# Second block of chunk 1 as seven block products, with chunk 0's feature tiles run through and two weight conversions exchanged

## The chip, the cores and the metric

The kernel runs on one core of a Trainium2 chip. The metric is device time in microseconds (us), the median of several runs. A core has a matrix engine (PE), a vector engine (DVE), a scalar engine (ACT), a general engine (POOL) and a queue for transfers (SP). Each works through its own instructions in the order of the program and waits for the others by semaphores. PE writes to PSUM banks; everything else lies in SBUF.

## The reference

Attention with sketched features, followed by a two-layer network on its result. For each head, features of 64 numbers are made from q and k, and the output of attention is a ratio of two products with sums over the sequence:

```python
def phi(x):
    a = np.einsum('rd,bhsd->bhsr', S1, x)
    b = np.einsum('rd,bhsd->bhsr', S2, x)
    return np.einsum('bhsi,bhsj->bhsij', a, b).reshape(*x.shape[:-1], r * r)
kv = np.einsum('bhsf,bhsd->bhfd', k_p, v)
z = np.sum(k_p, axis=2)
num = np.einsum('bhsf,bhfd->bhsd', q_p, kv)
den = np.einsum('bhsf,bhf->bhs', q_p, z)[..., None] + 1e-06
# (num / den) becomes x: 4352 tokens of 128 channels
h = x @ w_in                                   # 128 x 2048
g = 0.5 * h * (1.0 + erf(h * inv_sqrt2))
return (g @ w_out).astype(np.float32)          # 2048 x 128
```

Batch 4, heads 4, sequence 1088, head size 32. The weights of S1, S2, w_in and w_out arrive as float64; everything is computed in float32.

## The kernel before

**Chunks and feature tiles.** The tokens are cut into eight chunks of 512 (n = 0 to 7, two for each batch entry) and a ninth of 256 with the rests. The hidden layer has 16 tiles of 128 features (fi = 0 to 15). For one pair (n, fi) the function `hidden` makes one product of w_in's tile with the chunk's x on PE (L683, into one of two PSUM banks `h_ps`), and ACT takes the bank through Gelu into SBUF (L690). A PSUM bank can be written again only when its Gelu has read it, so the hidden product of a step waits for the Gelu of two steps before.

**Two ways of the second product.** "Usual" tiles are multiplied with w_out's tile one by one (`project`, L818, a product of 128x128 by 128x512) and accumulate in a PSUM bank `o_ps`; ACT later copies that sum away (`take_usual`, L795). The other tiles are taken in blocks of four: `two_products` (L767) makes seven block products instead of eight, in a scheme of Winograd's kind. They are issued as seven pairs of 64x256 products for two tiles and two halves. The block products need two kinds of sums made on POOL beforehand: `token_sums` (L732 to L735, four instructions over the Gelu outputs of the block, into tiles `bits_low`, `bits_a`, `bits_e`, `bits_m`) and `channel_sums(i)` (L719 to L722, four instructions over piece i of w_out). In the order of the pairs, names 4 and 7 use `bits_low`, 1 and 5 `bits_a`, 6a and 6b `bits_e`, and 2 and 3 `bits_m`. When a chunk's last block is done, `drain` (L775 to L788) recombines the products on ACT and DVE, and `store` writes the chunk out.

**Conversion of the weights.** w_in and w_out come in five pieces each, of 2, 2, 4, 4 and 4 feature tiles (`w_in_sb[0]` to `[4]`). A piece is converted from float64 words by `Rounding`: ACT scales the low words (L260); DVE cuts out the exponent field (L268) and the mantissa field (L273); ACT makes the exponent (L279); DVE makes the mantissa (L287), sets the sign (L292), and DVE or, for some pieces, POOL multiplies (L297). `round_at(t, w)` puts the first half of this into step t and the second half into step t + 1.

**The order of the work.** It is written out by hand. A list `steps` gives the pairs (n, fi) in turn; for step t the loop at the end issues the hidden product and Gelu of its pair, then `token_sums` if a block is complete, then what `at(t, ...)` has put into the slot of t, then the second products due at t. An engine keeps exactly this order. Two lists matter here: the one of steps, and the one of slots (L988 to L1050), which holds the conversions, the channel sums and the attention of the next batch entry: turning keys (`key_turn_blocks`, L359), features (`features_of_all` L934, `outer_of_all` L942 to L949), their sums (`add_tokens`, L958 to L964), `finish_keys` (L428), `turn_kv` (L458), `z_sum`, `query_sketch` (L568), `query_outer` (L580 to L603), `attend` (L617).

Before the change the steps are: chunk 0 fi 0 to 3, chunk 1 fi 0 to 3, chunk 0 fi 4 to 7, chunk 1 fi 4 to 7 (all usual, steps 0 to 15), then chunk 0 fi 8 to 15 (steps 16 to 23), chunk 1 fi 8 to 15 (24 to 31), and from step 32 on the other chunks, with all their tiles in blocks. The conversions stand at steps 4 (w_in, piece 2), 6 (w_out, 2), 8 (w_in, 3), 10 (w_out, 3), 12 (w_in, 4) and 14 (w_out, 4).

Of the kernel before, what the change touches and what calls it, by code (L numbers as in the profile page):

```python
# [16 lines left out]
def kernel(  # L17
# [18 lines left out]
    pe, dve, act, pool, sp = nc.tensor, nc.vector, nc.scalar, nc.gpsimd, nc.sync  # L36
# [5 lines left out]
    NF = d_ff // 128  # L42
# [7 lines left out]
    NCH = J // JC  # L50
    C = D + 1
    LAG = 2
    NMAIN = B * NCH
    NB = 4

    USUAL = 8
    NCHUNK = NMAIN + 1
    assert B == 4 and d_model == 128 == H * D == JC * D == 2 * F and H == 4 and REM == 64 and NCH == 2

# [34 lines left out]
    w_in_sb = [big.tile([d_model, c1 - c0], FP, name=f"w_in{i}") for i, (c0, c1) in enumerate(pieces)]  # L94
# [92 lines left out]
    for i, s in enumerate((S1, S2)):  # L187
        s, e = words(s)
# [266 lines left out]
    def turn_kv(b, banks):  # L455

        for rows in (slice(0, 64), slice(64, 128)):
            pe.matmul(banks[rows, 1, :128], lhsT=kv_T[b], rhs=ident, start=True, stop=True)  # L458
        act.copy(out=kz[b], in_=banks[:, 1, :128])
# [217 lines left out]
    def hidden(n, fi, by_halves=False):  # L677
        W = width[n]
        ps = first_banks.pop((n, fi)) if (n, fi) in first_banks else hidden_bank()
        w = w_tile(w_in_sb, fi)  # L680
        for rows in (slice(0, 64), slice(64, 128)) if by_halves else (slice(0, 128),):
            if (n, fi) not in begun:
                pe.matmul(ps[rows, :W], lhsT=w[:, rows], rhs=xT[n][:, :W], start=True, stop=True)  # L683
        if n < NCH and fi < USUAL:
            g_of[n, fi] = mlp.tile([128, CW], FP, name="g", bufs=4)
        else:
            if fi % NB == 0:
                blocks[n, fi // NB] = block(FP)
            g_of[n, fi] = blocks[n, fi // NB][:, fi % NB]
        act.activation(out=g_of[n, fi][:, :W], in_=ps[:, :W], func=ACT.Gelu)  # L690
# [58 lines left out]
        return sums[n, b][j][:, e], T[j][:, k]  # L749

    def first_block(n):
        return USUAL // NB if n < NCH else 0

    def two_products(n, b, i):

        fours, ones_, sixes = [("4", "7", e, e) for e in range(2)], [("1", "5", e, e) for e in range(2)], ("6a", "6b", 0, 1)

        opens = b == first_block(n)
        order = fours + ([sixes] + ones_ if opens else ones_ + [sixes]) + [("2", "3", e, e) for e in range(2)]
        two = order[i]  # L760
        if opens and i == 0:
            acc[n] = [out_bank(), out_bank()]
        for name, e in zip(two[:2], two[2:]):
            half, bank, col = PLACE[name]
            moving, fixed = factor(n, b, name, e)

            pe.matmul(acc[n][bank][half * 64:(half + 1) * 64, col:col + HW], lhsT=fixed, rhs=moving,  # L767
                      start=opens and e == 0 and name in "4715", stop=b == NF // NB - 1, skip_group_check=True)
# [24 lines left out]
    def take_usual(n):  # L793
        usual[n] = mlp.tile([128, CW], FP, name="g", bufs=4)
        act.copy(out=usual[n], in_=o_of[n])  # L795
# [9 lines left out]
        return N[:, 1]  # L805

    def project(n, fi, parts=range(B // 2)):
        first, final = fi == 0, fi == (USUAL if n < NCH else NF) - 1
        if first:
            o_of[n] = out_bank() if n < NMAIN else [work_bank() for i in range(B // 2)]  # L810
        g = g_of[n, fi]
        if n == NMAIN:

            for i in parts:
                pe.matmul(o_of[n][i][:, :128], lhsT=g[:, i * 128:(i + 1) * 128], rhs=w_tile(w_out_sb, fi),  # L815
                          start=first, stop=final)
            return
        pe.matmul(o_of[n], lhsT=w_tile(w_out_sb, fi), rhs=g, start=first, stop=final)  # L818
# [65 lines left out]
    late = []  # L884
# [32 lines left out]
    w_out[0].fields()  # L917


    steps = [(n, fi) for f in range(0, USUAL, 4) for n in range(NCH) for fi in range(f, f + 4)]  # L920
    steps += [(n, fi) for n in range(NCHUNK) for fi in range(USUAL if n < NCH else 0, NF)]
    slots = {t: [] for t in range(len(steps) + LAG)}

    def at(t, f, *a):
        slots[t].append(lambda: f(*a))
# [40 lines left out]
    held = {}  # L966
# [21 lines left out]
    def round_at(t, w, product_by=dve):  # L988
        r = []
        at(t, lambda: (r.append(Rounding(w)), r[0].low_words(), r[0].fields()))  # L990
        at(t + 1, lambda: (r[0].exponents(), r[0].mantissas(), r[0].signs(), r[0].product(product_by)))

    for i, (t0, t1) in enumerate(((4, 6), (8, 10))):
        round_at(t0, w_in_sb[i + 2])
        round_at(t1, w_out_sb[i + 2])
    round_at(12, w_in_sb[4], pool)
    at(13, channel_sums, 3)

    at(12, widen_v_rem, 1)
    for r in range(2):  # L1000
        at(14, key_turn_blocks, 1, r)
    round_at(14, w_out_sb[4], pool)
    at(15, query_turn, 2)
    at(16, features_of_all, 1)
    at(16, outer_of_all, 1)
    at(16, turn_keys_rem, 1)
    at(17, features_rem, 1)
    at(17, add_tokens, 1)
    at(18, channel_sums, 4)

    at(21, finish_keys, 1, False)
    at(22, lambda: turn_kv(1, held["kv"]))
    at(23, z_sum, 1)
    at(23, fold_z, 1)
    at(23, query_turn, 3)
    at(24, query_sketch, 2)
    at(24, query_outer, 2)
    for i, t in enumerate((25, 26, 28)):
        at(t, channel_sums, i)
    at(11, spread_sketches)  # L1020
    at(40, repeat_first_z)
# [32 lines left out]
    done = {t: [] for t in range(len(steps) + LAG + 1)}  # L1054
    drains = {t: [] for t in range(len(steps) + LAG + 1)}
    for t, (n, fi) in enumerate(steps):
        if n < NCH and fi < USUAL:
            products[t + LAG].append((project, n, fi))
            if fi == USUAL - 1:
                slots[t + LAG + 1 + 2 * n].append(lambda n=n: take_usual(n))  # L1060
        elif n == NMAIN:
            at_ = max(t + LAG, (n * NF + 5) if fi < 3 else (n * NF + 6) if fi < 5 else 0)
            if fi < NF - 4:
                products[at_].append((project, n, fi))
            if fi == NF - 1:

                products[at_] += [(project, n, NF - f, (i,)) for f, i in ((4, 0), (3, 0), (2, 0), (4, 1), (1, 0), (3, 1),
                                                                          (2, 1), (1, 1))]
                done[at_ + 1].append(n)
        elif fi % NB == NB - 1:  # L1070
            b = fi // NB
            opens = b == first_block(n)
            late = int(n < NCH or n == NCH and opens)
            for later, pairs in ((3, 3), (4, 2), (5, 2)) if opens else ((2, 2), (3, 2), (4, 1), (5, 2)):
                later += late
                for i in range(pairs):
                    products[t + later].append((two_products, n, b, len([p for q in products.values() for p in q
                                                                        if p[:3] == (two_products, n, b)])))
            if b == NF // NB - 1:
                drains[t + 6 + late].append(n)  # L1080
                done[t + 12].append(n)

    for t in range(len(steps) + LAG):
        if t < 4:

            hidden(0, t)
            if t == 1:
                w_out[0].low_words()
                w_out[0].exponents()
                w_out[0].finish()  # L1090
                w_out[1].fields()
            if t == 2:
                w_out[1].low_words()
            if t == 3:
                banks = work_banks()
                numerators_by_token(1, halves(banks), range(JC))
                w_out[1].mantissas(by_pool=True)
                w_out[1].exponents()
                divide(1, banks, range(JC), by_head_pair=False)
                w_out[1].signs()  # L1100
                w_out[1].product()
                for u in range(4):
                    for f, *a in products[u]:
                        f(*a)
            continue
        if t == 4:
            for i, copy in enumerate((by_act, by_dve)):
                turn_half(1, i, work_bank(), copy)
            first_hidden(1, 0)
            for f, *a in products[t]:  # L1110
                f(*a)
            first_hidden(1, 1)
        for n in drains[t]:
            drain(n)
        if t < len(steps):
            n, fi = steps[t]
            hidden(n, fi, by_halves=t >= 18 and (n < NMAIN or fi < 5))
        if t < len(steps) and steps[t][0] < NMAIN and steps[t][1] % NB == NB - 1:
            n, b = steps[t][0], steps[t][1] // NB
            if b >= first_block(n):  # L1120
                token_sums(n, b)
        for f in slots[t]:
            f()
        for n in done[t]:
            store(n)
        if t != 4:
            for f, *a in products[t]:
                f(*a)
# [41 lines left out]
```

## Time and profile before

| what | value |
|---|---|
| device time, median of 3 runs | 262.52 us (262.11 to 262.53) |
| the profiled execution's own time | 261.87 us |
| its span, first to last instruction | 260.1 us |
| PE busy | 255.2 us, 98% of the span |
| POOL busy | 163.4 us, 63% |
| DVE busy | 152.2 us, 59% |
| ACT busy | 114.6 us, 44% |
| granted PE clock | full in all slices |

The profile is of one execution. Its page gives the busy time of each engine, the span in 40 slices with a digit of tenths, the chain of work that ended last, and the costliest groups of instructions. A row of the timeline gives start, duration, engine, line of the kernel, operation, output and inputs, shape and count, and in brackets the idle time of the engine just before with what ended it. The rows' durations overlap a little on one engine, so the time from one start to the next is the better price of an instruction. All times are us from the start of the span. A matmul on float32 shows as two records; two products on the two halves of PE's columns run side by side.

The steps that the change touches lie between 29 and 75 us. Step t = 8 (chunk 0, fi 4) begins on PE at 29.20, step 16 at 42.94 and step 20 at about 49.4.

### The profile page before, as it was taken

Reading aid. Unit: us, or ns where it says so; the run is one execution under the profiler, and the core shown is the slowest. Engines: PE = TensorE matmul, PEld = TensorE weight load, DVE = VectorE, ACT = ScalarE, POOL = GpSimd, SP = SyncE. Lnnn points to the kernel's source line nnn. Section 1 sums busy time; section 2 is a strip of 40 time slices with the busy share of each in tenths; the row PEclk is TensorE's granted clock in tenths of the full one; section 3 lists DMA queues with packets and bytes.
Section 4 is the critical chain, followed back from the end, with each engine's and each line's share of the span. In section 5 each row is a group of like instructions: output and inputs, shape, how many; then the busy total and the mean of one; then the engine's idle time right before and its main releaser. Section 6 shows DMA issues by size and latency. Waiting matters only on the chain.

```text
span 260.1 us, 5738 instructions
## 1 busy us (share of the span) xinstructions
PE 255.2 (98%) x2331; PEld 132.6 (51%) x2331; DVE 152.2 (59%) x315; ACT 114.6 (44%) x219; POOL 163.4 (63%) x173
## 2 busy tenths in 40 slices
PE   8999999999999999999999999999999999999994
PEld 6845444344444554444444454454445444445794
DVE  3895878969798997680278957630664043600330
ACT  4674767532535334533334334533352335333441
POOL 3403007799968777687758865967778776877200
PEclk9999999999999999999999999999999999999999
DMA  6479857810000101001000011020001000110020
GB/s 206 138 223 366 193 126 204 203 25 9 3 0 15 28 4 28 12 13 30 3 0 3 0 27 16 4 40 0 4 0 28 15 4 0 19 24 0 3 40 20
DMA packets 29530, 13.48 MB, mean 52 GB/s; under 512 B 21824, under 2 KB 27712, under 8 KB 29504
## 3 DMA queue, kind: packets, MB, share of 16 engines
q1 hardware_dynamic: 29472, 13.12, 20.6%
q8 instruction: 18, 0.29, 0.5%
q14 instruction: 8, 0.07, 0.1%
q10 hardware_dynamic: 32, 0.00, 0.0%
HBM read 10.88 MB, written 2.23 MB: 50 GB/s over the span
## 4 chain that ended last, share of the span: by engine, by line
PE 96%; DVE 1%; DMA 1%; ACT 1%; issue 0%; ACTq 0%; DVEq 0%
PE h_ps L683 45%; PE o_ps L767 33%; PE o_ps L818 5%; PE w_ps L815 3%; PE w_ps L428 2%; PE w_ps L617 1%; PE w_ps L568 1%; PE h_ps L697 1%; DMA raw_SR<-in_S_dram 1%; PE o_ps L417 1%; PE w_ps L934 1%; PE w_ps L635 0%; PE w_ps L534 0%; DVE x_tok L656 0%; PE w_ps L333 0%; PE h_ps L635 0%
## 5 line engine op out<-in xcount | busy, mean ns | idle before, releaser
L683 PE MATMUL h_ps<-xT,w_in 128*64 128x512 f32 (+3 forms) x514 | 137.3, 576 | 0.0
L690 ACT ACTIVATE block<-h_ps 128x512 f32<-128x512 f32 (+1 forms) x128 | 73.1, 571 | 121.4 <-PE h_ps L683 120.9
L767 PE MATMUL o_ps<-block,w_out 128*64 128x256 f32 x224 | 57.5, 379 | 0.0
L683 PEld LDWEIGHTS h_ps<-xT,w_in 128*64 128x64 f32 (+1 forms) x514 | 41.8, 142 | 29.5 <-issue 11.6
L732 POOL TENSOR_TENSOR bits_low<-block 128x512 f32<-128x512 f32 x28 | 35.7, 1274 | 27.6 <-ACT block L690 27.6
L767 PEld LDWEIGHTS o_ps<-block,w_out 128*64 128x64 f32 x224 | 30.5, 137 | 37.5 <-issue 26.8
L733 POOL TENSOR_TENSOR bits_a<-block 128x512 f32<-128x512 f32 x28 | 35.8, 1278 | 13.4 <-ACT block L690 13.4
L734 POOL TENSOR_TENSOR bits_e<-bits_a,block 128x512 f32<-128x512 f32 x28 | 36.1, 1291 | 2.2
L735 POOL TENSOR_TENSOR bits_m<-block,bits_e 128x512 f32<-128x512 f32 x28 | 35.9, 1281 | 2.2
L580 DVE STREAM_TRANSPOSE w_ps<-w_ps 128x512 f32<-128x512 f32 (+1 forms) x7 | 4.9, 693 | 42.7 <-PE w_ps L568 30.3
L767 PE MATMUL o_ps<-block,small 128*64 128x256 f32 x112 | 29.3, 384 | 0.0
L767 PE MATMUL o_ps<-bits_low,small 128*64 128x256 f32 x112 | 29.2, 384 | 0.0
L767 PE MATMUL o_ps<-bits_a,small 128*64 128x256 f32 x112 | 28.8, 379 | 0.0
L767 PE MATMUL o_ps<-bits_m,w_out 128*64 128x256 f32 x112 | 28.7, 379 | 0.0
L767 PEld LDWEIGHTS o_ps<-block,small 128*64 128x64 f32 x112 | 14.5, 136 | 18.9 <-issue 9.1
L782 DVE COPY sums<-o_ps 64x256 f32<-64x256 f32 x8 | 3.3, 417 | 34.7 <-PE o_ps L767 34.7
L767 PE MATMUL o_ps<-bits_e,small 128*64 128x256 f32 x112 | 17.1, 384 | 0.0
L818 PE MATMUL o_ps<-g,w_out 128*128 128x512 f32 x32 | 16.3, 597 | 0.0
L767 PEld LDWEIGHTS o_ps<-bits_m,w_out 128*64 128x64 f32 x112 | 15.3, 137 | 0.0
L767 PEld LDWEIGHTS o_ps<-bits_a,small 128*64 128x64 f32 x112 | 15.2, 137 | 0.0
L767 PEld LDWEIGHTS o_ps<-bits_low,small 128*64 128x64 f32 x112 | 14.5, 137 | 0.0
L767 PEld LDWEIGHTS o_ps<-bits_e,small 128*64 128x64 f32 x112 | 7.5, 136 | 10.5 <-issue 9.1
(181 smaller groups left out, 299.4 us busy)
## 6 DMA issues: line engine op xcount, KB each, us to landing
out_dram<-oT SPq DMA_DIRECT2D x26, 64.0 KB, 2.2
block<-in_moe_w_in_dram SPq DMA_DIRECT2D x3, 512.0 KB, 7.2
block<-in_moe_w_out_dram SPq DMA_DIRECT2D x3, 512.0 KB, 11.0
k<-in_k_dram SPq DMA_DIRECT2D x12, 128.0 KB, 2.8
v<-in_v_dram SPq DMA_DIRECT2D x12, 128.0 KB, 3.1
q<-in_q_dram SPq DMA_DIRECT2D x24, 64.0 KB, 2.3
k<-in_k_dram SPq DMA_DIRECT2D x2, 256.0 KB, 2.9
q<-in_q_dram SPq DMA_DIRECT2D x2, 256.0 KB, 3.7
```

The source lines that it names most:

```text
L428: pe.matmul(ps[h * D:(h + 1) * D, part * F:(part + 1) * F], lhsT=lhsT, rhs=features, start=start, stop=stop, skip_group_check=True)
L580: dve.transpose(out=tok, in_=ps[:, :, :H2])
L683: pe.matmul(ps[rows, :W], lhsT=w[:, rows], rhs=xT[n][:, :W], start=True, stop=True)
L690: act.activation(out=g_of[n, fi][:, :W], in_=ps[:, :W], func=ACT.Gelu)
L732: pool.tensor_sub(out=s[3], in0=a11, in1=a21)
L733: pool.tensor_add(out=s[1], in0=a21, in1=a22)
L734: pool.tensor_sub(out=s[2], in0=s[1], in1=a11)
L735: pool.tensor_sub(out=s[4], in0=a12, in1=s[2])
L767: pe.matmul(acc[n][bank][half * 64:(half + 1) * 64, col:col + HW], lhsT=fixed, rhs=moving, start=opens and e == 0 and name in "4715", stop ...
L782: dve.tensor_copy(out=N[lo, 0, one], in_=a0[lo, one])
L815: pe.matmul(o_of[n][i][:, :128], lhsT=g[:, i * 128:(i + 1) * 128], rhs=w_tile(w_out_sb, fi), start=first, stop=final)
L818: pe.matmul(o_of[n], lhsT=w_tile(w_out_sb, fi), rhs=g, start=first, stop=final)
```

## The change

1. `USUAL` becomes a list: chunk 0 keeps eight usual tiles, chunk 1 has four. Chunk 1's fi 4 to 7 is now a block of seven products.
2. The steps become: chunk 0 fi 0 to 3, chunk 1 fi 0 to 3, chunk 0 fi 4 to 15 (steps 8 to 19), chunk 1 fi 4 to 15 (steps 20 to 31). Chunk 0's fi 8 is thus at step 12 and its fi 12 at step 16, four steps earlier each.
3. The second products of chunk 0's fi 4 to 7 are spread over steps 10, 12, 14 and 16; its blocks' products start at steps 20 and 22, with the pairs 1 and 5 ahead of 6a and 6b.
4. w_in's piece 4 is converted at step 10 (with POOL's multiplication at 11), w_out's piece 3 at step 12, which was the other way round.
5. `channel_sums(2)` moves from step 28 to step 9, `channel_sums(3)` from 13 to 14. On POOL, piece 2's sums and w_in piece 4's multiplication now stand ahead of `spread_sketches` and `widen_v_rem(1)`.
6. The attention of the next batch entry moves one to two steps later in the list: features from 16 to 18, `finish_keys` from 21 to 22, `query_sketch(2)` and `query_outer(2)` from 24 to 26. Chunk 0 is drained at step 26 rather than 30 and stored at 31 rather than 35.
7. The hidden products are issued by halves of 64 columns from step 17 rather than 18.

```diff
--- before.py
+++ after.py
@@ -53,7 +53,7 @@
     NMAIN = B * NCH
     NB = 4
 
-    USUAL = 8
+    USUAL = [8, 4]
     NCHUNK = NMAIN + 1
     assert B == 4 and d_model == 128 == H * D == JC * D == 2 * F and H == 4 and REM == 64 and NCH == 2
 
@@ -681,7 +681,7 @@
         for rows in (slice(0, 64), slice(64, 128)) if by_halves else (slice(0, 128),):
             if (n, fi) not in begun:
                 pe.matmul(ps[rows, :W], lhsT=w[:, rows], rhs=xT[n][:, :W], start=True, stop=True)
-        if n < NCH and fi < USUAL:
+        if n < NCH and fi < USUAL[n]:
             g_of[n, fi] = mlp.tile([128, CW], FP, name="g", bufs=4)
         else:
             if fi % NB == 0:
@@ -749,14 +749,14 @@
         return sums[n, b][j][:, e], T[j][:, k]
 
     def first_block(n):
-        return USUAL // NB if n < NCH else 0
+        return USUAL[n] // NB if n < NCH else 0
 
     def two_products(n, b, i):
 
         fours, ones_, sixes = [("4", "7", e, e) for e in range(2)], [("1", "5", e, e) for e in range(2)], ("6a", "6b", 0, 1)
 
         opens = b == first_block(n)
-        order = fours + ([sixes] + ones_ if opens else ones_ + [sixes]) + [("2", "3", e, e) for e in range(2)]
+        order = fours + ([sixes] + ones_ if opens and n else ones_ + [sixes]) + [("2", "3", e, e) for e in range(2)]
         two = order[i]
         if opens and i == 0:
             acc[n] = [out_bank(), out_bank()]
@@ -805,7 +805,7 @@
         return N[:, 1]
 
     def project(n, fi, parts=range(B // 2)):
-        first, final = fi == 0, fi == (USUAL if n < NCH else NF) - 1
+        first, final = fi == 0, fi == (USUAL[n] if n < NCH else NF) - 1
         if first:
             o_of[n] = out_bank() if n < NMAIN else [work_bank() for i in range(B // 2)]
         g = g_of[n, fi]
@@ -917,8 +917,8 @@
     w_out[0].fields()
 
 
-    steps = [(n, fi) for f in range(0, USUAL, 4) for n in range(NCH) for fi in range(f, f + 4)]
-    steps += [(n, fi) for n in range(NCHUNK) for fi in range(USUAL if n < NCH else 0, NF)]
+    steps = [(n, fi) for n in range(NCH) for fi in range(4)]
+    steps += [(n, fi) for n in range(NCHUNK) for fi in range(4 if n < NCH else 0, NF)]
     slots = {t: [] for t in range(len(steps) + LAG)}
 
     def at(t, f, *a):
@@ -990,32 +990,34 @@
         at(t, lambda: (r.append(Rounding(w)), r[0].low_words(), r[0].fields()))
         at(t + 1, lambda: (r[0].exponents(), r[0].mantissas(), r[0].signs(), r[0].product(product_by)))
 
-    for i, (t0, t1) in enumerate(((4, 6), (8, 10))):
-        round_at(t0, w_in_sb[i + 2])
-        round_at(t1, w_out_sb[i + 2])
-    round_at(12, w_in_sb[4], pool)
-    at(13, channel_sums, 3)
+    round_at(4, w_in_sb[2])
+    round_at(6, w_out_sb[2])
+    round_at(8, w_in_sb[3])
+    round_at(10, w_in_sb[4], pool)
+    round_at(12, w_out_sb[3])
+    at(9, channel_sums, 2)
+    at(14, channel_sums, 3)
 
     at(12, widen_v_rem, 1)
     for r in range(2):
         at(14, key_turn_blocks, 1, r)
     round_at(14, w_out_sb[4], pool)
     at(15, query_turn, 2)
-    at(16, features_of_all, 1)
-    at(16, outer_of_all, 1)
-    at(16, turn_keys_rem, 1)
-    at(17, features_rem, 1)
-    at(17, add_tokens, 1)
+    at(18, features_of_all, 1)
+    at(18, outer_of_all, 1)
+    at(18, turn_keys_rem, 1)
+    at(19, features_rem, 1)
+    at(19, add_tokens, 1)
     at(18, channel_sums, 4)
 
-    at(21, finish_keys, 1, False)
-    at(22, lambda: turn_kv(1, held["kv"]))
-    at(23, z_sum, 1)
-    at(23, fold_z, 1)
-    at(23, query_turn, 3)
-    at(24, query_sketch, 2)
-    at(24, query_outer, 2)
-    for i, t in enumerate((25, 26, 28)):
+    at(22, finish_keys, 1, False)
+    at(23, lambda: turn_kv(1, held["kv"]))
+    at(24, z_sum, 1)
+    at(24, fold_z, 1)
+    at(24, query_turn, 3)
+    at(26, query_sketch, 2)
+    at(26, query_outer, 2)
+    for i, t in enumerate((25, 26)):
         at(t, channel_sums, i)
     at(11, spread_sketches)
     at(40, repeat_first_z)
@@ -1054,10 +1056,11 @@
     done = {t: [] for t in range(len(steps) + LAG + 1)}
     drains = {t: [] for t in range(len(steps) + LAG + 1)}
     for t, (n, fi) in enumerate(steps):
-        if n < NCH and fi < USUAL:
-            products[t + LAG].append((project, n, fi))
-            if fi == USUAL - 1:
-                slots[t + LAG + 1 + 2 * n].append(lambda n=n: take_usual(n))
+        if n < NCH and fi < USUAL[n]:
+            to = t + LAG + max(fi - NB, 0)
+            products[to].append((project, n, fi))
+            if fi == USUAL[n] - 1:
+                slots[to + 1 + 2 * n].append(lambda n=n: take_usual(n))
         elif n == NMAIN:
             at_ = max(t + LAG, (n * NF + 5) if fi < 3 else (n * NF + 6) if fi < 5 else 0)
             if fi < NF - 4:
@@ -1070,7 +1073,7 @@
         elif fi % NB == NB - 1:
             b = fi // NB
             opens = b == first_block(n)
-            late = int(n < NCH or n == NCH and opens)
+            late = int(n < NCH or n == NCH and opens) + int(n == 0 and opens)
             for later, pairs in ((3, 3), (4, 2), (5, 2)) if opens else ((2, 2), (3, 2), (4, 1), (5, 2)):
                 later += late
                 for i in range(pairs):
@@ -1114,7 +1117,7 @@
             drain(n)
         if t < len(steps):
             n, fi = steps[t]
-            hidden(n, fi, by_halves=t >= 18 and (n < NMAIN or fi < 5))
+            hidden(n, fi, by_halves=t >= 17 and (n < NMAIN or fi < 5))
         if t < len(steps) and steps[t][0] < NMAIN and steps[t][1] % NB == NB - 1:
             n, b = steps[t][0], steps[t][1] // NB
             if b >= first_block(n):
```

## The prediction

> **What bounds the kernel now.** I read the page first: engines' busy time, the granted clock, the chain that ended last.
>
> ```profile
> PE 255.2 (98%) x2331; PEld 132.6 (51%) x2331; DVE 152.2 (59%) x315; ACT 114.6 (44%) x219; POOL 163.4 (63%) x173
> PEclk9999999999999999999999999999999999999999
> PE 96%; DVE 1%; DMA 1%; ACT 1%; issue 0%; ACTq 0%; DVEq 0%
> ```
>
> PE is the bound over the whole span, at full clock, and 96% of the last chain. So a gain must be PE work removed, and any wait of PE made in the middle stays in the total, as no idle PE time behind it can absorb it. The list of PE's waits has three, 1.2 us together, all before 24 us.
>
> Then the timeline of PE from 40 to 75 us, for prices:
>
> ```profile
> 42.08 1.02 PE L818 MATMUL o_ps<-g,w_out 128*128 128x512 f32 x2
> 42.94 1.02 PE L683 MATMUL h_ps<-xT,w_in 128*128 128x512 f32 x2
> ...
> 47.54 3.81 PE L683 MATMUL h_ps<-xT,w_in 128*64 128x512 f32 x16
> 51.28 1.10 PE L428 MATMUL w_ps<-k_p,v 128*32 128x64 f32 x64
> ```
>
> Start to start, a usual product or a hidden one takes 0.86. Four hidden products with nothing between (47.54 to 51.28) took 3.74 instead of 3.44: about 0.1 is the turn to narrower products behind them, 0.2 waits on Gelu. In the same view two pairs of block products (eight records) start at 62.87 and the next product at 63.73: 0.43 a pair.
>
> Last, DVE, POOL and ACT around the conversions:
>
> ```profile
> 37.99 0.42 DVE L268 TENSOR_SCALAR bits_e<-block 128x512 uint32<-128x512 uint32 x1
> 38.33 0.42 DVE L273 TENSOR_SCALAR bits_a<-block 128x512 uint32<-128x512 uint32 x1
> ...
> 40.70 1.30 DVE L359 STREAM_TRANSPOSE kT<-k 128x512 f32<-128x512 f32 x2
> 41.92 0.51 DVE L268 TENSOR_SCALAR bits_e<-block 128x512 uint32<-128x512 uint32 x1
> 42.35 0.68 DVE L273 TENSOR_SCALAR bits_a<-block 128x512 uint32<-128x512 uint32 x1
> ```
> ```profile
> 42.10 0.63 POOL L719 TENSOR_TENSOR small<-w_out 128x128 f32<-128x128 f32 x1
> ...
> 45.02 1.27 POOL L297 TENSOR_TENSOR w_out<-bits_m,bits_e 128x512 f32<-128x512 f32 x1
> 46.37 0.46 POOL L719 TENSOR_TENSOR small<-w_out 128x128 f32<-128x128 f32 x1
> ...
> 49.34 1.28 POOL L732 TENSOR_TENSOR bits_low<-block 128x512 f32<-128x512 f32 x1 [1.16 <-ACT block L690]
> ...
> 54.54 1.27 POOL L732 TENSOR_TENSOR bits_low<-block 128x512 f32<-128x512 f32 x1
> ```
> ```profile
> 42.77 0.71 ACT L279 ACTIVATE bits_r<-bits_e,below 128x512 uint32<-128x512 uint32 x1
> 44.00 0.60 ACT L690 ACTIVATE block<-h_ps 128x512 f32<-128x512 f32 x1 [0.51 <-PE h_ps L683]
> ```
>
> DVE's L268 and L273 are longer beside POOL's channel sums (0.51 and 0.68) than alone (0.42). Channel sums took 2.92 beside them (42.10 to 45.02), and 1.8 from 46.37. A block's token sums take 5.2 (49.34 to 54.54).
>
> [...] A DVE addition of two SBUF tiles (L801) took 1.38 at 76.72, beside POOL's L732 that ended at 77.83, and 0.37 in the shortest of its eight runs. L273 above ends 0.3 after POOL's L719. [...] here such a turn costs 0.09 to 0.15 (42.94 to 43.89 for a hidden product followed by narrow ones).
>
> **The change part by part.**
>
> *PE work.* Four usual products are 4 x 0.86 = 3.44, seven pairs 7 x 0.43 = 3.01: 0.43 less. The back-to-back hidden products go, as usual products now stand between them: about 0.2 less. The other turns of width are as many as before within one, 0.1. Sum: -0.6.
>
> *POOL work.* One block of token sums more, 5.2 us.
>
> *w_in's piece 3 for step 12.* PE without waits reaches step 12 at 35.21: from 29.20, six products of 0.86 for steps 8 to 10 and one for step 11. The conversion ended at 34.63; now channel sums of piece 2, released at about 31.28 by w_out's piece, run beside it. As in the pair of views above they cost DVE short waits, most covered by ACT's L279, the last about 0.1: ready at 34.75. No wait, with 0.4 to spare; 0 to 0.3 if that is short. w_in's piece 4 is ready at 38.8 and wanted at 40.36: hidden.
>
> *First wait: ACT.* PE runs on to step 16 at 40.36, step 17 at about 42.2 (a usual product lies between) and step 18 at 43.1. Step 18 needs the Gelu of step 16. Ahead of that Gelu on ACT stands L279 of w_out's piece 4, put into step 15, and it needs DVE's L268. DVE's order before it: w_in's last L292 at 36.65 (after ACT's L279, 35.90), L268 of w_out's piece 3 at 37.26, L273, L287, L292, L297, two transposes, L268. Start to start these rows are 0.61, 0.34, 0.52, 0.69, 0.72, 0.61 and 1.22 apart (36.65 to 41.92), 4.7 in all, which puts L268 at 41.4 if nothing is waited for, or 42.0 if L292 waits for ACT's L279, which stands behind a Gelu. But POOL's multiplication of w_in (1.28) is released at 37.42, [...] and holds L273 from 37.6 to 38.8; then eight small POOL instructions (`spread_sketches`, `widen_v_rem`: 2.2 us from their rows at 20.8 to 22.8 and 36.5) alternate with L287, L292 and L297. I put w_out's piece 3 at 41.1, the transposes at 41.0 to 42.15, L268 at 42.15 to 42.5, L279 at 42.5, the Gelu at 43.15 to 43.75 (0.6 from L279's start, as in earlier rows), PE's step 18 at 43.9 instead of 43.1. **+0.8**; [...] 1.2 if each small instruction bites fully. Queued behind it on ACT are the next Gelus and chunk 0's `take_usual`.
>
> *Second wait: POOL.* PE from step 18 to the first pair of block 3 of chunk 0: hidden and turn 0.95, L934 0.59, L333 and turn 0.32, hidden 0.86, L399 and turns 0.4, hidden 0.86, three pairs 1.29, hidden 0.86, two pairs 0.86, hidden and turn 0.95, L428 1.14, two pairs 0.86: 9.94, so at 53.85. It wants channel sums of w_out's piece 4 and `bits_low` of that block. POOL is now full from 37.4: small ones until 42.2, channel sums 3 (2.9, beside the conversion as before) to 45.1, token sums of block 2 (5.2) to 50.25, only then w_out's multiplication (1.3; it now stands behind them) to 51.5, channel sums 4 (1.8) to 53.3, L732 (1.28) to 54.6, seen by PE at 54.75. **+0.9**[...]. The pairs after it (`bits_a` at 55.8, `bits_e` at 57.2, `bits_m` at 58.5) come later than these: hidden.
>
> *The rest.* The changed program's instruction order does hold the seven pairs and four token sums in the new places. DVE's keys chain ends (L964) at 54.5, wanted by `z_sum` at 58.3: hidden. The drain of chunk 0 (3.3 us from L782 at 66.96) now stands ahead of `query_outer(2)` (6.4 us, 57.83 to 64.25) on DVE; the two fill some 9.8 us of the 10.2 in which PE goes from the drain's start at about 60.9 to `attend(2)` at 71.2. Hidden by 0.3; if that is short, 0 to 0.4. Token sums of the new block (58.5 to 63.6) are ahead of PE's need at 63.4 (`bits_low` at 59.7) and 64.2 (`bits_e` at 62.3). Chunk 0's stores are issued earlier on SP, which waits 20.0 us for them before: nothing.
>
> Sum against the profiled execution: -0.6 + 0.8 + 0.9 = +1.1, and 0.1 for the two margins: 261.87 + 1.2 = 263.1. The median lies 0.65 above that execution: 262.52 + 1.2 = **263.7 us**.
>
> **The rivals.**
>
> *The arithmetic gain stands* (261.9). The one mechanism: ACT's L279 for w_out's piece 4 gets its exponent field 0.8 earlier than I think, so that step 18 doesn't wait, and POOL's queue is then short by as much. It decides if L268 begins by 41.35. For it: in the list DVE's work up to there isn't more than before, only in another order. Against: before, that L268 began at 41.92, with POOL mostly idle until 40.86, and its predecessors hang on ACT's order. 262.52 - 0.6 = 261.9.
>
> [...] (262.4 to 262.9). Then only 0.5 of the first wait is left and POOL comes in time: -0.6 + 0.5 = -0.1 to +0.35 with the turns. Against: L801 and the channel sums' rows.
>
> *More waits* (264.6). [...] 1.2 + 1.2, with `attend(2)` or w_in's piece 3 late: +2.1. For: both margins are under 0.5.
>
> **How the numbers follow.** Mine 0.58, with its own range 263.1 to 264.3; the gain stands 0.07; [...] 0.17; more waits 0.18. A measurement of this kernel can tell about 0.2%, 0.53 us, from no change. Faster: the second, 0.07. Same: most of the third, 0.15. Slower: the rest, 0.78. The range reaches from the low side of the third to the upper of the last, 262.3 to 264.8, leaving the gain and a worse pile of waits outside.
>
> **What would show it.** In the changed profile: PE's list of waits has a hidden product on Gelu (L690) near 43 to 44, and a block product (L767) on POOL's L732 near 54 to 55, 0.5 to 1.2 each; ACT idles before an L279 of about 42.5 for DVE's L268; DVE has an L273 near 37.6 that takes about 1.5; POOL has no idle time from 38 to 58; PE's busy time is some 0.5 less while the span is longer. The prediction is wrong if PE shows neither wait, or if a transfer or the late attention shows instead.

## The result, and the profile after

The changed kernel takes 266.5 us, median of 6 runs (264.57 to 268.3), against 262.52 before: a ratio of 1.0155, 95% interval 1.0127 to 1.0182. It is slower by 4.0 us, not by the 1.2 forecast, and outside the range. The profiled execution took 266.52, its span 264.7.

The lines of the page of the changed kernel that answer to the first ones shown of before:

```profile
PE 257.8 (97%) x2353; PEld 133.8 (51%) x2353; DVE 155.9 (59%) x315; ACT 114.3 (43%) x219; POOL 170.8 (65%) x177
PEclk9999999799999999999999999999999999999999
PE 84%; DMA 5%; SPq 5%; DVE 2%; ACT 1%; issue 1%; POOL 0%; DVEq 0%; ACTq 0%
```

PE is busy 2.6 longer than before, although it was given less to do. The clock row tells most of the reason: its eighth slice (46.3 to 52.9) has a 7, so the same products took longer there, 1.5 in all, as is worked out below. Another 0.4 is a wait that the profile counts as busy (keys_early, below), and 0.6 lies ahead of step 11. Only 84% of the last chain is PE now. The top of the list of PE's waits in the changed kernel (us in total, times, longest) has one that was not there before:

```profile
PE h_ps L683 <- ACT block L690: 2.0, 1, 2.0
```

The timeline of PE in the changed kernel, around that wait:

```profile
42.86 1.08 PE L683 MATMUL h_ps<-xT,w_in 128*64 128x512 f32 x4
45.92 1.97 PE L683 MATMUL h_ps<-xT,w_in 128*64 128x512 f32 x4 [1.98 <-ACT block L690]
47.82 1.11 PE L934 MATMUL w_ps<-kT,S_ab 64*32 64x256 f32 x16
```

Step 18's hidden product would follow step 17's at 43.72 and starts at 45.92: 2.2 lost. Then it takes 1.97 instead of 1.08, and L934 1.11 instead of the 0.66 that the same sixteen products took without such a wait ahead of them. The view by stretches (length, PE's busy time and records, granted clock, DMA share, GB/s) gives the clock:

```profile
46.00:48.00 2.00, 2.00 (x12) 0.50 0.85 222
48.00:50.00 2.00, 2.00 (x21) 0.66 0.83 238
```

After the 1.98 in which PE stood still, 3.41 us of products, from 45.94 to 49.35, ran at a granted clock of 0.50. The other engines of the changed kernel in the same time, DVE first, then POOL, then ACT:

```profile
43.06 1.51 DVE L268 TENSOR_SCALAR bits_e<-block 128x512 uint32<-128x512 uint32 x1
```
```profile
43.00 0.45 POOL L719 TENSOR_TENSOR small<-w_out 128x128 f32<-128x128 f32 x1
43.42 0.45 POOL L720 TENSOR_TENSOR small<-w_out 128x128 f32<-128x128 f32 x1
43.83 0.45 POOL L721 TENSOR_TENSOR small<-w_out,small 128x128 f32<-128x128 f32 x1
44.36 0.52 POOL L722 TENSOR_TENSOR small<-w_out,small 128x128 f32<-128x128 f32 x1
```
```profile
44.66 0.72 ACT L279 ACTIVATE bits_r<-bits_e,below 128x512 uint32<-128x512 uint32 x1 [2.81 <-DVE bits_e L268]
45.29 1.06 ACT L690 ACTIVATE block<-h_ps 128x512 f32<-128x512 f32 x2
```

This is the predicted chain, link for link: L268 of w_out's piece 4, ACT's L279, the Gelu, step 18. But L268, which takes 0.42 alone, took 1.51. It came 0.06 after POOL's first channel sum of piece 3 and stayed through three of them, which follow each other every 0.41 to 0.42; it ended 0.3 after the third, with a gap of 0.08 in POOL's row there. That gap lies ahead of L722, the first of the four that needs the result of the one just before it.

**Where the 4.0 us are.** PE's products can be laid end to end, start to start, over the whole rest of the program. In the profile of before, PE goes from the start of step 11's hidden product (34.35) to that of its last product in 222.0. Of the changed kernel and of the experiments below, the parts of that stretch are in the table (us, worked out from PE's starts). Its marks are the hidden product of step 17, the features of the next batch entry (the first L934), the product of its keys and values (kv_sum, L428 of `finish_keys`), `z_sum`, and the features of the batch entry after it (the second L934). The median stands beside its difference to the kernel before, as that was timed on the same occasion. (From z_sum to the second L934 it is 13.22 in all of them, and step 11 to step 17 is 7.82, or 7.73 where step 17 is of full width, in full_width, all_four and kv_between.)

| kernel | median; difference to before | step 17 to L934 | L934 to kv_sum (L428) | kv_sum to z_sum | second L934 to the end |
|---|---|---|---|---|---|
| the changed kernel | 266.5; +4.0 | 4.96 | 7.73 | 5.82 | 186.45 |
| filled | 265.0; +2.6 | 4.39 | 7.11 | 5.82 | 186.45 |
| gap_early | 263.86; +1.8 | 3.26 | 7.11 | 6.15 | 186.46 |
| spread_early | 264.17; +1.7 | 3.20 | 7.11 | 5.82 | 186.46 |
| field_first | 264.32; +1.9 | 1.87 | 7.11 | 7.59 | 186.46 |
| both | 263.54; +1.1 | 1.90 | 7.11 | 6.71 | 186.45 |
| keys_early | 262.77; +0.4 | 1.87 | 7.11 | 6.67 | 186.05 |
| dve_product | 263.45; +1.1 | 1.89 | 7.88 | 5.82 | 186.45 |
| full_width | 263.46; +1.1 | 2.00 | 6.77 | 7.01 | 186.46 |
| all_four | 262.98; +0.6 | 2.03 | 7.84 | 5.82 | 186.05 |
| kv_between | 262.10; -0.4 | 2.04 | 7.63 | 5.11 | 186.04 |

With hidden products by halves, the least values sum to 7.82 + 1.87 + 7.11 + 5.82 + 13.22 + 186.05 = 221.9: without any wait the changed program gains 0.1. Over that, the changed kernel has 3.09 + 0.62 + 0.40 = 4.1. Of the first two, 3.7 together, 2.2 is the wait and 1.5 the clock after it. Sum: +4.0, which is the difference of the medians. The span of this one execution is longer by 4.6, because its steps up to 11 were also 0.7 late (step 11 at 35.04): 0.2 of that is there by 5.2, and 0.5 comes in the middle of a product at 12.1 (L635), for which the profile names no releaser. That is no part of the change: gap_early, the same program up to there, had step 11 at 34.19.

### The profile page after: what moved, and what is told of

It reads as the page before. It is cut to its first block, busy times and chain, and to the rows that moved or that the text cites. A ratio compares the mean times of both kernels' runs of the same rounds, so it can differ in the third digit from the quotient of the medians.

```text
span 264.7 us, 5788 instructions
## 1 busy us (share of the span) xinstructions
PE 257.8 (97%) x2353; PEld 133.8 (51%) x2353; DVE 155.9 (59%) x315; ACT 114.3 (43%) x219; POOL 170.8 (65%) x177
## 4 chain that ended last, share of the span: by engine, by line
PE 84%; DMA 5%; SPq 5%; DVE 2%; ACT 1%; issue 1%; POOL 0%; DVEq 0%; ACTq 0%
PE h_ps L683 39%; PE o_ps L767 34%; DMA block<-in_moe_w_out_dram 4%; PE w_ps L815 3%; PE w_ps L428 1%; PE w_ps L617 1%; PE w_ps L568 1%; SPq L121 1%; PE w_ps L848 1%; SPq L173 1%; SPq L132 1%; DMA v<-in_v_dram 1%; PE w_ps L934 1%; SPq L106 1%; PE h_ps L333 1%
## 5 line engine op out<-in xcount | busy, mean ns | idle before, releaser
L690 ACT ACTIVATE block<-h_ps 128x512 f32<-128x512 f32 (+1 forms) x132 | 75.3, 571 | 124.0 <-PE h_ps L683 123.4
L767 PE MATMUL o_ps<-block,w_out 128*64 128x256 f32 x232 | 59.8, 379 | 0.0
L732 POOL TENSOR_TENSOR bits_low<-block 128x512 f32<-128x512 f32 x29 | 37.1, 1280 | 28.2 <-ACT block L690 28.2
L733 POOL TENSOR_TENSOR bits_a<-block 128x512 f32<-128x512 f32 x29 | 37.5, 1292 | 13.6 <-ACT block L690 13.6
L734 POOL TENSOR_TENSOR bits_e<-bits_a,block 128x512 f32<-128x512 f32 x29 | 37.7, 1299 | 2.3
L735 POOL TENSOR_TENSOR bits_m<-block,bits_e 128x512 f32<-128x512 f32 x29 | 37.1, 1279 | 2.3
L767 PE MATMUL o_ps<-bits_a,small 128*64 128x256 f32 x116 | 30.0, 379 | 0.0
L767 PE MATMUL o_ps<-bits_m,w_out 128*64 128x256 f32 x116 | 29.8, 379 | 0.0
L818 PE MATMUL o_ps<-g,w_out 128*128 128x512 f32 x24 | 12.2, 596 | 0.0
```

What stands on the lines that cost most here:

```text
L732: pool.tensor_sub(out=s[3], in0=a11, in1=a21)
L733: pool.tensor_add(out=s[1], in0=a21, in1=a22)
L734: pool.tensor_sub(out=s[2], in0=s[1], in1=a11)
L735: pool.tensor_sub(out=s[4], in0=a12, in1=s[2])
```

## The experiments

**Is it the clock? (filled)** On the changed kernel, five products of zeros, into a bank that features use next, keep PE busy where it waits for the Gelu. The output is unchanged.

```diff
-        ps = work_banks()
+        ps = held.pop("warm", None) or work_banks()
...
+    def warm(n):
+        held["warm"] = work_banks()
+        keep_busy(n, held["warm"][:, 0])
+
+    at(17, warm, 5)
```

> The changed kernel with five products of zeros (128x128 by 128x256, 0.43 us each) put on PE behind step 17's hidden product, where PE stood still for 2.0 us. Nothing else waits for them; the output is the same. Clock theory (the wait of 2 us itself lowers PE's clock afterwards, and that is what most of the runs lost beyond the wait): the granted clock is 1.0 in the records, the narrow products behind step 18 (L934) take 0.6 and not 1.0 us, and the time is about that of the one undisturbed run, 264.5 to 265.3 us (the filling and two turns of width may stand 0.2 longer than the wait). Rival (the clock falls for another reason, such as the mix of the new products, or the loss lies elsewhere): the time stays at 266 to 267 and the clock below 1.0.

265.0 us (ratio to before 1.0091, 1.0069 to 1.0114), 1.5 less than without the filling. L268 took 1.52 again and the Gelu came as late; the fillers even ran on 0.3 longer than the wait. But from 44 to 50 the granted clock was 1.00, and L934 to kv_sum took 7.11 instead of 7.73. A line of the view by stretches of this kernel (PE, weight loads, DVE, ACT, POOL, then the clock):

```profile
46.00:48.00 2.00, 2.00 (x23) 0.44 (x22) 2.00 (x2) 1.47 (x3) 2.00 (x2) 1.00 0.86 238
```

So the wait's aftermath is the clock's, and is worth about 1.5.

**What held L268? (gap_early)** If L268 gets done only where POOL's row has a gap, the order of POOL's four sums decides how long it takes. Only that order is changed, for piece 3; the sums are the same.

```diff
-        pool.tensor_sub(out=t3, in0=b22, in1=b12)
-        pool.tensor_sub(out=t2, in0=b22, in1=t1)
-        pool.tensor_sub(out=t4, in0=b21, in1=t2)
+        pool.tensor_sub(out=t3, in0=b22, in1=b12) if i != 3 else pool.tensor_sub(out=t2, in0=b22, in1=t1)
+        pool.tensor_sub(out=t2, in0=b22, in1=t1) if i != 3 else pool.tensor_sub(out=t4, in0=b21, in1=t2)
+        pool.tensor_sub(out=t4, in0=b21, in1=t2) if i != 3 else pool.tensor_sub(out=t3, in0=b22, in1=b12)
```

> Built on the changed kernel itself (266.5, wait of step 18 for its Gelu 2.0). Only the order of the four instructions of piece 3's channel sums differs: sum, the one that depends on it, the one that depends on that, and the free one last, where the free one was second. In the changed kernel DVE's L268 of w_out's piece 4, begun at 43.06 against POOL's sums, took 1.51 and ended in the gap ahead of the fourth sum, the first that needs the result of the one just before it. Theory [...]: the gap now lies ahead of the second sum, L268 ends 0.8 earlier and takes about 0.7, the wait of step 18 falls to 1.2, the clock stays full, 264.2. Rival ([...] L268 waits for something else): L268 still takes 1.5, the wait is 2.0, 266.5.

263.86 us (1.0071, 1.0055 to 1.0087), by the place of one instruction on POOL: 2.6 less than the changed kernel by the medians, 2.2 with each set beside its own timing of before. In the timelines of this kernel, POOL and then DVE:

```profile
42.17 0.45 POOL L719 TENSOR_TENSOR small<-w_out 128x128 f32<-128x128 f32 x1
42.69 0.52 POOL L720 TENSOR_TENSOR small<-w_out,small 128x128 f32<-128x128 f32 x1
43.29 0.52 POOL L721 TENSOR_TENSOR small<-w_out,small 128x128 f32<-128x128 f32 x1
```
```profile
42.22 0.68 DVE L268 TENSOR_SCALAR bits_e<-block 128x512 uint32<-128x512 uint32 x1
```

L268 begins 0.05 after POOL's first sum, as in the changed kernel, and now takes 0.68. It ends 0.28 after the first sum's end, as it ended 0.29 after the third's in the changed kernel, and each time the sum that came next needed the one just before it. The longest wait of PE in its list is 1.2, for the same Gelu, and the clock stays full. Both numbers are the theory's; had a time or a count of POOL's instructions decided, 1.51 and 2.0 would have stayed. (The total gains more than the 0.8 of L268, since the wait of 1.2 did not cost the clock: its mean was 1.0, against 0.993.)

That is shown for this run of sums. It does not hold everywhere, as rows of the changed kernel, DVE and then POOL, tell:

```profile
45.27 1.57 DVE L287 SCALAR_TENSOR_TENSOR bits_m<-bits_a,bits_low 128x512 f32<-128x512 uint32 x1
```
```profile
44.84 1.44 POOL L732 TENSOR_TENSOR bits_low<-block 128x512 f32<-128x512 f32 x1
46.24 1.71 POOL L733 TENSOR_TENSOR bits_a<-block 128x512 f32<-128x512 f32 x1
```

L287 (0.69 alone) ended at 46.84, 0.56 after L732, and L733, which ran on until 47.95, took 1.71 instead of 1.28. But L733 does not need L732's result, and there is no gap between the two. In the same way L273 of before (42.35 to 43.03) ended 0.30 after L719 (42.10 to 42.73), while L720 ran (42.70, 0.64 instead of 0.45); these two do not depend on each other. In both cases POOL's instruction ahead had itself taken longer (L732 1.44 instead of 1.28, L719 0.63 instead of 0.45), and L719 of piece 3 in the changed kernel had not (0.45). What decides where there is no gap was not tried, and by what way an instruction of POOL's makes one of DVE's longer, no view shows.

**Take the collision away (spread_early, field_first, both).** spread_early issues POOL's eight small instructions at step 8; field_first cuts out the two fields of w_out's piece 4 (L268, L273) ahead of two key transpositions (1.22) on DVE; both has both edits.

```diff
-    at(11, spread_sketches)
+    at(8, spread_sketches)
```
```diff
+    round_at(14, w_out_sb[4], pool)
     for r in range(2):
         at(14, key_turn_blocks, 1, r)
-    round_at(14, w_out_sb[4], pool)
```

> The changed kernel with one edit: spread_sketches (eight small POOL instructions) at step 8 and not 11, so that POOL does it before channel_sums(2), while it is idle. [...] piece 3's channel sums start when w_out's piece 3 is ready (about 41) and alternate with DVE's transposes, so L268 takes 0.4 to 0.6 and not 1.5, the Gelu of step 16 comes about 1 us earlier, PE waits 0.8 to 1.2 instead of 2.0 and the time is 262.9 to 265. Rival (DVE's own length sets it): the wait stays at 2.0 and the time at 266.5.

264.17 us (1.0055, 1.0034 to 1.0076). L268 began at 43.22 and took 0.51; PE's wait is 1.1, the clock full.

> The changed kernel with one edit: w_out's piece 4 has its two fields (L268, L273) cut out ahead of the two key transposes on DVE (1.2 us) and not behind them. ACT theory (step 18 waits for a Gelu that stands behind L279, which waits for L268): L279 is free about 1.2 us earlier or more, PE's wait on Gelu falls from 2.0 to below 0.5, the clock stays at 1.0, and what is left is the predicted wait for POOL's bits_low near 54, 0.5 to 1.0: time 263 to 264. Rival (the wait comes from POOL through something else than L268): the wait on Gelu stays near 2.0 and the time near 266.5.

264.32 us (1.0064, 1.0043 to 1.0085). L268 began at 41.27 and took 0.46; step 18 does not wait for its Gelu any more. But what the first wait had hidden comes out: kv_sum to z_sum takes 7.59, 1.77 more than without a wait, because PE is now ahead of POOL. The expectation had 0.5 to 1.0 for it.

> Both edits at once: spread_sketches at step 8, and w_out piece 4's fields ahead of the transposes. [...] no wait on Gelu is left, POOL is up to 1 us earlier, its bits_low is late for PE by 0.5 at most, the clock stays at 1.0, and the time is 262.0 to 263.0: about that of the kernel before. If the 0.6 us that the change removes from PE are real and POOL is in time, 261.9. Rival (the new blocks cost PE more than they save): 263.5 or more with no wait in the profile.

263.54 us (1.0035, 1.0026 to 1.0045). With POOL's small instructions earlier, too, this second wait is 0.89 (6.71 against 5.82), at the place where the prediction put it. At most 0.5 was expected here, and the total is above the 262.0 to 263.0 expected. The timeline of PE, and POOL's row that it waits for, in this kernel:

```profile
53.44 0.59 PE L767 MATMUL o_ps<-block,small 128*64 128x256 f32 x2
54.28 0.43 PE L767 MATMUL o_ps<-bits_low,small 128*64 128x256 f32 x1 [0.25 <-POOL bits_low L732]
```
```profile
52.95 1.27 POOL L732 TENSOR_TENSOR bits_low<-block 128x512 f32<-128x512 f32 x1
```

The bracket says 0.25, and the list of waits 0.2. Yet the second half of the pair stood still from 53.44 to 54.28: the first half of the columns had gone on with two products alone, so PE did not count as idle. The distance from kv_sum to z_sum shows what the wait costs.

**What is left (keys_early, dve_product, full_width, all_four).** All are built on both. The first turns the next keys at step 22 instead of 28, the second lets DVE multiply w_out's piece 4, the third makes hidden products by halves from step 20 only, and the last has all three.

```diff
-                at(t - 3 if n > 3 else t - 4, key_turn_blocks, b, r)
+                at(t - 3 if n > 3 else t - 10, key_turn_blocks, b, r)
```
```diff
-    round_at(14, w_out_sb[4], pool)
+    round_at(14, w_out_sb[4])
```
```diff
-            hidden(n, fi, by_halves=t >= 17 and (n < NMAIN or fi < 5))
+            hidden(n, fi, by_halves=t >= 20 and (n < NMAIN or fi < 5))
```

> Built on the kernel with both edits (spread_sketches at step 8, fields of w_out's piece 4 ahead of the key transposes), 263.54. Here the transposes of batch entry 2's first keys stand at step 22 instead of 28, ahead of chunk 0's drain and query_outer(2) on DVE. Theory (features_of_all(2) waits for them about 0.43): the gap from L934 at step 31 to the product behind it falls from about 1.9 to about 1.45, the total to 263.1. Rival (that gap comes from a turn of width or from PE's own order): no change, 263.5.

262.77 us (1.0012, 0.9997 to 1.0028). In the timeline of PE, L934 at the next batch entry's features and the product behind it, in the changed kernel and then here:

```profile
74.58 1.05 PE L934 MATMUL w_ps<-kT,S_ab 64*32 64x256 f32 x16
75.56 0.43 PE L767 MATMUL o_ps<-block,w_out 128*64 128x256 f32 x1
```
```profile
71.78 0.64 PE L934 MATMUL w_ps<-kT,S_ab 64*32 64x256 f32 x16
72.35 0.43 PE L767 MATMUL o_ps<-block,w_out 128*64 128x256 f32 x1
```

0.98 becomes 0.57, as before the change: 0.41 was a wait in the middle of L934 for DVE's two transpositions. The list of waits shows nothing of it in the changed kernel, whose L934 only seems longer. Against both, with each beside its own timing of before, the gain is 0.7; the starts show 0.4 of it, and the rest was not located.

> Built on the kernel with both edits, 263.54. Here DVE, not POOL, multiplies w_out's piece 4, which takes an instruction of 1.3 out of POOL's full queue. Theory (the block products of chunk 0's block 3 wait about 0.95 because POOL's queue up to bits_low is too long by that): that wait goes, 262.6, unless the later keys on DVE then hold kv_sum (L428) by up to 0.7, which leaves 263.3. Rival (the wait is for the block's last Gelu, and POOL isn't late): the block products still wait, 263.5.

263.45 us (1.0037, 1.0022 to 1.0052), the same as both. POOL is in time now, but the other possibility of the expectation came true: DVE's keys are late, and the list of waits of this kernel has one of 0.7, of L428 for DVE's L404.

> Built on the kernel with both edits, 263.54. Here hidden products are made by halves from step 20 instead of 17, so that the full-width products L333 and L399 at steps 18 and 19 stand among full-width hidden products. Theory (turns of width cost about 0.35 more than before the change): PE reaches block 3's products 0.35 earlier, but there it waits for POOL, so the total falls by 0 to 0.1 only (263.4 to 263.5) and the wait for bits_low grows by about 0.3. Rival (POOL's end isn't what PE waits for): 263.2.

263.46 us (1.0043, 1.0027 to 1.0059), no change in the total, as expected: L934 to kv_sum is 0.34 shorter and kv_sum to z_sum 0.30 longer. So turns of width do cost 0.34 in the changed kernel, and what is saved there is waited for POOL.

> The kernel with both edits, and the three further ones of this group together: key transposes at step 22, w_out's piece 4 multiplied by DVE, hidden products by halves from step 20. Theory (both waits, the late keys and the turns of width are all that the change lost): 263.54 - 0.95 - 0.43 - 0.35 = 261.8, faster than before by the 0.6 of PE work, or 262.5 if kv_sum waits 0.7 for DVE. Rival (something else is lost with the change): 263 or more.

262.98 us (1.0025, 1.0008 to 1.0042), above the 261.8 to 262.5 of the theory. The sum of the three is not had: with PE faster, kv_sum waits 1.07 for DVE (7.84 against 6.77).

**The wait for DVE (kv_between).** Built on all_four.

```diff
-    at(15, query_turn, 2)
+    at(20, query_turn, 2)
...
-    at(22, finish_keys, 1, False)
...
+    products[22].insert(2, (finish_keys, 1, False))
```

> Built on the kernel with all four edits (262.98), where kv_sum (L428) waits 1.07 at 51.0 for DVE's L404. Here batch entry 1's finish_keys is issued after step 22's two pairs of block 2 instead of ahead of them, 0.86 later on PE, and the query transposition L519 (0.63) moves on DVE from step 15 to step 20, behind the features. Theory (DVE's chain of keys is late by 1.07, and nothing else is lost): L404 comes at 51.0, PE wants it at 51.9, bits_low of block 3 is ready at 53.1 and wanted at 53.0; the wait goes and the total is 261.9, 0.5 below before: the removed PE work, seen at last. Rival (POOL's bits_low of block 3 is then late in its turn, since its other sums follow DVE's longer chain): 262.5 to 263.

262.10 us; the ratio to before is 0.9985, 0.9971 to 1.0. No wait for Gelu, POOL or DVE is left in its list, and the stretch from step 11 to the end is 221.8 against 222.0 of before. Its median is the lowest of the kernels, 0.36 below before, but its interval just reaches 1, so that it is faster than before is not shown. The 0.5 expected were not had: step 11 to L934 takes 9.76, where field_first has 9.69, and L934 to z_sum 12.74, where the least values of the two parts give 6.77 + 5.82 = 12.59.

**A last one (last_usual).** Built on kv_between, with the last usual product between the hidden ones of steps 17 and 18.

```diff
-            to = t + LAG + max(fi - NB, 0)
+            to = t + LAG + max(fi - NB, 0) + (fi == 7)
```

> Built on the kernel with kv_sum between the two blocks (262.1). Here the usual product of chunk 0's fi 7 stands behind the hidden product of step 17 instead of 16, so that step 18's hidden product no longer follows step 17's at once. Theory (step 17 to L934 takes 2.04 instead of 1.81 because step 18 waits for the Gelu of step 16, a back-to-back loss that the prediction had taken for removed): step 18 comes after the Gelu's end at 43.4, the stretch shrinks by 0.2, the total to 261.9. Rival (ACT's later order, take_usual behind the Gelus, delays features instead): 262.1 or more.

262.17 us (0.9995, 0.9976 to 1.0014). From step 15 to L934 PE took 4.60 here and 4.61 in kv_between: nothing is gained. Step 17 to L934 takes 2.04 in kv_between, where a product of 0.86 and one with a turn of 0.95 would give 1.81; that these 0.2 come from the two standing next to each other is refuted. In both kernels step 18 starts 0.05 after the end of step 16's Gelu, which stands behind ACT's L279; that this is the cause is likely but was not tried.

## Why the prediction was wrong

It forecast slower, by two waits, at 0.58. The direction was right, but not by the sum that gave it: one of the two waits did not come, and the other, with the clock behind it, was more than four times its size. Measured, the terms are 2.2 for the first wait, 1.5 for the clock, nothing for the second wait, 0.4 for attention and -0.1 for PE's work, 4.0 together. The steps:

- **PE work, -0.6: too much.** The pairs are cheaper as it said, but 0.34 of it goes to turns of width: the full-width L333 and L399 now stand among narrow products, as full_width shows, while the step counted the turns "as many as before within one". Without waits the changed program gains 0.1, and kv_between 0.2. Of the difference, 0.6 - 0.34 - 0.1, nearly 0.2 was not located.
- **w_in's pieces 3 and 4 hidden: right.** From step 11 to step 17 PE takes 7.82 in the changed kernel, nine products of 0.86 and a turn (7.73 where step 17 is of full width).
- **First wait, +0.8: the step that failed.** Place, chain and start were right: L268 forecast at 42.15, and found at 43.06, of which 0.7 is this execution's late start. Its length was not: 0.35 to 0.7 was taken from rows in which L268 and L273 stood beside channel sums, 1.51 is what it took. The step knew such a length (it forecast 1.5 for L273 beside one long POOL instruction, and 1.50 came), but thought that short instructions alternate. Here they did not: L268, begun at 43.06, stayed through three, of which L720 and L721 began after it, at 43.42 and 43.83; in gap_early, with the gap ahead of the second sum, it took 0.68. The term measured 2.2.
- **No term for the clock: missing, 1.5.** After the idle time of 2.0 the clock was 0.50 for 3.41 us, and after that of 1.2 in gap_early it stayed full. filled shows the whole sum: with PE kept busy there the clock was 1.00 and the time 1.5 less. Not every run lost it, as the six runs of the changed kernel differ: one kept full clock and took 264.57, 1.9 below the median, and the slowest, 268.3, had a mean clock of 0.986, twice the loss of the others' 0.993. What sets the runs apart was not tried.
- **Second wait, +0.9: POOL's time right, the wait hidden.** `bits_low` of block 3 was forecast for 54.6 and came at 55.35, of which 0.7 is the late start. But PE, held up by 3.7, came to that block's products after it, so the changed kernel doesn't have this wait. In field_first, where the first wait is gone, it is 1.77, the sum of the 0.8 and 0.9 forecast within 0.1. That it is 0.89 in both is chance: there PE is early and so is POOL.
- **Attention hidden by 0.3: wrong, +0.4.** The step counted the drain and `query_outer(2)` ahead of `attend(2)` on DVE, and left out the key transpositions behind them, which L934 needs; keys_early shows 0.41.

Of the rivals, "more waits" came closest with 264.6. But of its mechanisms the second wait was not there, the first was there at nearly twice its upper end, and in place of `attend(2)` the features behind it were late. "The gain stands" and the rival of 262.4 to 262.9, which left 0.5 of the first wait, are refuted by L268 itself, with 1.51.

## What to carry to other kernels

What an instruction loses beside another engine can be longer than that engine's instruction: here DVE's L268 took 1.51 instead of 0.42 and stayed through a run of three sums of 0.45 on POOL, up to the next gap, and with a dependent pair put early in the run it took 0.68. A wait of PE can have a second price, the clock after it, which here came with an idle time of 2.0 and not with 1.2, and added two thirds (1.5 to 2.2). And a wait that is removed lets PE run into the next one (1.77 in field_first), so the sum of waits has to be made along PE's time, with each engine's queue set against it, which the list of waits alone does not give.

## What the runs showed of the hardware

- DVE's L268, 0.42 alone, ended only after three POOL instructions that followed every 0.41 to 0.42, in the changed kernel (1.51) and in filled (1.52). With a dependent instruction second it took 0.68 (gap_early). Ahead of an independent POOL instruction, without a gap, DVE's L287 ended 0.56 after L732 in the changed kernel, where L732 had itself taken longer (1.44 instead of 1.28).
- A PE idle time of 2.0 was followed by 3.41 us at a clock of 0.50 in the profiled run of the changed kernel, and keeping PE busy there gained 1.5 (filled); of its six runs five had a mean clock of 0.986 to 0.994 and one of 1.0. Idle times of 1.1 and 1.2 (spread_early, gap_early) were not, with a clock of 1.00 in their profiles.
- A pair of products on the two column halves can hide a wait: 0.84 by the starts, 0.25 by the record (both, at 54.28). So can a group of products that starts in time and waits inside (L934 in the changed kernel, 0.41).
